# Rows of x directly ahead of the next chunk's scores in TensorE's order, from the third block on

## Chip, cores, metric

One core of a Trainium2 chip. The metric is the device time of one execution in microseconds (us); a ratio always compares kernels that ran on the same chip in the same rounds.

## The reference

A gated linear attention (4 batches, 8 heads, 768 tokens, head size 48) feeds a feed-forward block with an unusual activation:

```python
f = 1/(1+exp(-f_logit))
for t in range(S):                                   # 768 tokens
    state = f[t][:, None] * state + outer(k[t], v[t])
    y[t]  = q[t] @ state
x = y as (3072 tokens, 384)
h = x @ w_in                                         # 384 -> 2048
g = h * erf(max(h,0) + log1p(exp(-|h|)))
out = g @ w_out                                      # 2048 -> 384
```

## The kernel before

Tokens are taken in 24 chunks of 128; three chunks make one of 8 blocks, numbered 0 to 7 in the code (the "third block" is `blk == 2`, chunks 6 to 8). While the feed-forward matmuls of block `it` and `it - 2` run on TensorE as a stream of "slots" (one 128x384 program matmul each, 0.645 us), the attention of block `it + 1` is dropped in between, in four stages per chunk:

- `stage_d` (decays): one matmul `ps_d`; ScalarE exps `dp` and `kd`; VectorE makes `qd`, GpSimd makes `kd`
- `stage_t`: 8 transposes `ps_t`, copied to `qT` and `kT`
- `stage_s` (scores): 8 matmuls `sc`, masked by VectorE into `A`; 8 matmuls `dS`; VectorE and GpSimd update the state `Mbd`
- `stage_y` (rows of x): 28 program matmuls (16 in the first chunk of a batch), with 32 output columns each, copied to `xT`

In the traces the engines take their instructions in program order. The parts (cut):

```python
def prepare(blk, j0, j1):          # gates of a whole block
    nc.vector.tensor_scalar(out=lt, in0=lt, scalar1=LOGIT_MIN, ..., op0=ALU.max)
    nc.scalar.activation(out=lt, in_=lt, func=AF.Exp, scale=-1.0)
    nc.scalar.activation(out=lt, in_=lt, func=AF.Ln, bias=1.0)
...
def stages(blk):
    g0 = blk * CPB
    todo = [(stage_d, g0), (stage_t, g0)] if blk == 1 else []
    for g in range(g0, g0 + CPB):
        last = g == n_chunks - 1
        todo += [] if last else [(stage_d, g + 1)]
        todo += [(stage_s, g)]
        todo += [] if last else [(stage_t, g + 1)]
        todo += [(stage_y, g)]
    return todo
...
for it in range(n_blocks + 2):
    blk = it + 1
    todo = deque(stages(blk) if blk < n_blocks else [])
    n = n_slots[it]                            # 48, 48, then 96
    at = [int(3 + (n - 13) / max(1, len(todo)) * i) for i in range(len(todo))]
    for s, _ in enumerate(slots(it)):          # one large matmul per slot
        ...                                    # weight rounding steps (VectorE), loads
        if at and s == at[0]:
            at.pop(0); f, g = todo.popleft(); f(g)
        ...                                    # a step of the activation
        if it + 2 < n_blocks and s == (16 if it < 2 else n // 2):
            prepare(it + 2, 0, CPB)
```

In `hidden()` the copies of hidden values out of PSUM are made by ScalarE for `blk < 2` and by VectorE after that. In the profiles `hps` are the hidden values as the matmuls write them, `Hg` their copy, `ops` the output sums. In PSUM, where the matmuls write, there are two buffers for `hps` and `ops` and two ("at") that `ps_d`, `ps_t` (twice), `dS` and `y` share in turn.

Of the kernel before, what the change touches and what calls it, by code (L numbers as in the profile page):

```python
# [38 lines left out]
FP32 = mybir.dt.float32  # L39
# [4 lines left out]
ALU = mybir.AluOpType  # L44
# [24 lines left out]
P = 128  # L69
# [3 lines left out]
def kernel(  # L73
# [11 lines left out]
    B, H, S, D = q.shape  # L85
# [5 lines left out]
    HP = H // 2  # L91
# [3 lines left out]
    CPB = 3  # L95
    TB = CPB * P
    n_blocks = B * S // TB
    n_chunks = B * NCH
# [23 lines left out]
    def rows(r, n=D):  # L122
        return slice(DP * r, DP * r + n)
# [3 lines left out]
    def y_matmuls(y, A, vt, qT, Mbd):  # L127

        for kt in range(n_k):
            todo = []  # L130
            for i in range(P // M):
                a, part = divmod(kt * (P // M) + i, 3)
                pair = vt[:, a].rearrange("p r d -> p (r d)")
                heads_in = {0: (0,), 1: (0, 1), 2: (1,)}[part]
                start = {0: 0, 1: M, 2: DP + D - M}[part]
                terms = []
                for r in heads_in:
                    o = D if (part == 1 and r == 1) else start
                    terms.append((pair[:, o : o + M], A[:, r, a, :]))
                if Mbd is not None:  # L140
                    flat = Mbd[:, a].rearrange("p r d -> p (r d)")
                    terms.append((flat[:, M * part : M * (part + 1)], qT[:, a, :]))
                todo.append(terms)
            for n in range(max(len(t) for t in todo)):
                for i, terms in enumerate(todo):
                    if n < len(terms):
                        nc.tensor.matmul(  # L147
                            y[M * i : M * (i + 1), kt, :], lhsT=terms[n][0], rhs=terms[n][1],
                            start=(n == 0), stop=(n == len(terms) - 1), skip_group_check=True,
                        )  # L150
# [17 lines left out]
    work1 = main.enter_context(tc.tile_pool(name="work1", bufs=1))  # L168
# [20 lines left out]
    def load_f(g):  # L189
        b, c = divmod(g, NCH)  # L190
        blk, j = divmod(g, CPB)
        if j == 0:
            lts[blk] = lpool.tile([P, CPB, d_model], FP32, name="lt", tag="lt")
        nc.sync.dma_start(
            out=lts[blk][:, j, :].rearrange("t (h d) -> t h d", d=D), in_=heads(f_logit, b, c)
        )
# [120 lines left out]
    def keep_busy(n):  # L317

        for _ in range(n):
            nc.tensor.matmul(busy[-1], lhsT=tri[:], rhs=tri[:], start=True, stop=True)  # L320
# [48 lines left out]
    def stage_s(g):  # L369
        b, c = divmod(g, NCH)  # L370
        qT, kT = qTs[g], kTs.pop(g)
        sc = ps_sc.tile([P, 2, HP, P], FP32, name="sc", tag="sc")
        for a in range(HP):
            for r in range(2):
                nc.tensor.matmul(  # L375
                    sc[:, r, a, :], lhsT=kT[rows(r), a, :], rhs=qT[rows(r), a, :],
                    start=True, stop=True,
                )
        if g in totals:

            pairs = dps[g % 2][:].rearrange("t (a r) d -> t a (r d)", r=2)
            for a in range(HP):
                nc.tensor.matmul(
                    totals[g][:, a : a + 1], lhsT=pairs[:, a, :], rhs=ident[:, P - 1 : P],
                    start=True, stop=True,
                )
            nc.vector.tensor_copy(out=Tall[:, g, :], in_=totals.pop(g))
        A = work1.tile([P, 2, HP, P], FP32, name="A", tag="A")
        nc.vector.tensor_tensor(  # L389
            out=A[:].rearrange("s r a t -> s (r a) t"),  # L390
            in0=sc[:].rearrange("s r a t -> s (r a) t"),
            in1=tri[:].unsqueeze(1).broadcast_to((P, H, P)),
            op=ALU.mult,
        )
        As[g] = A
        if c == NCH - 1:
            return
        dS = ps_at.tile([P, HP, D], FP32, name="dS", tag="at")
        vt, kd = vts[g % NV], kds[g % 2]
        for a in range(HP):  # L400
            for r in range(2):
                h = 2 * a + r
                nc.tensor.matmul(  # L403
                    dS[rows(r), a, :], lhsT=kd[:, h, 0:D], rhs=vt[:, a, r, 0:D],
                    start=True, stop=True,
                )
        new, old = Mbds[g % 2], Mbds[(g + 1) % 2]
        Sn = work1.tile([P, HP, D], FP32, name="Sn", tag="Sn")
        for r in range(2):
            total = Tall[rows(r), g, :].unsqueeze(2).broadcast_to((D, HP, D))  # L410
            if c == 0:
                nc.vector.tensor_tensor(
                    out=new[rows(r), :, r, :], in0=dS[rows(r)], in1=total, op=ALU.mult
                )
                continue
            nc.vector.tensor_tensor(  # L416
                out=Sn[rows(r)], in0=dS[rows(r)], in1=old[rows(r), :, r, :], op=ALU.add
            )
            nc.gpsimd.tensor_tensor(  # L419
                out=new[rows(r), :, r, :], in0=Sn[rows(r)], in1=total, op=ALU.mult  # L420
            )

    def stage_y(g):
        c = g % NCH
        blk, j = divmod(g, CPB)
        if j == 0:
            xTs[blk] = work.tile([P, n_k, TB], FP32, name="xT", tag="xT")
        if blk == 0:
            keep_busy(3)
        y = ps_at.tile([P, n_k, P], FP32, name="y", tag="at")  # L430
        y_matmuls(y, As.pop(g), vts[g % NV], qTs.pop(g), Mbds[(g + 1) % 2] if c else None)
        nc.scalar.copy(out=xTs[blk][:, :, j * P : (j + 1) * P], in_=y[:])  # L432


    acts = deque()
# [108 lines left out]
    def slots(it):  # L544

        if it >= n_blocks:
            return project(it - 2)
        made = [hidden(it, gi) for gi in range(n_g)]
        return chain(*made) if it < 2 else chain(*made[:2], project(it - 2), *made[2:])
# [20 lines left out]
    with tc.manual_schedule():  # L570
# [13 lines left out]
        for g in range(CPB, 2 * CPB):  # L584
# [3 lines left out]
            out=tri[:], in_=tri[:], pattern=[[1, P]], compare_op=ALU.is_ge, fill=0.0,  # L588
# [32 lines left out]
        def load_more():  # L621
            if to_load and home_free(to_load[0]):
                load_piece(to_load.pop(0))
# [51 lines left out]

        def stages(blk):
            g0 = blk * CPB
            todo = []
            if blk == 1:
                todo = [(stage_d, g0), (stage_t, g0)]  # L680
            for g in range(g0, g0 + CPB):
                last = g == n_chunks - 1
                todo += [] if last else [(stage_d, g + 1)]
                todo += [(stage_s, g)]
                todo += [] if last else [(stage_t, g + 1)]
                todo += [(stage_y, g)]
            return todo

        check = check_decays()
# [1 line left out]
        for it in range(n_blocks + 2):  # L691
            blk = it + 1
            if it + 2 < n_blocks:
                for j in range(CPB):
                    load_f((it + 2) * CPB + j)
            todo = deque(stages(blk) if blk < n_blocks else [])
            n = n_slots[it]
            at = [int(3 + (n - 13) / max(1, len(todo)) * i) for i in range(len(todo))]
            for s, _ in enumerate(slots(it)):
                due += 1 if it == 0 and s < 36 else 0.75  # L700
                while due >= 1:
                    weights_step()
                    due -= 1
                if s % 6 == 3:
                    load_more()
                if at and s == at[0]:
                    at.pop(0)
                    f, g = todo.popleft()
                    f(g)
                    if f is stage_y:  # L710
                        load_to(g + LOOK)
                if it == 0:
                    step = s >= 16 and s % 8 == 4
                elif it == 1:
                    step = s % 8 == 4
                elif it == 2:
                    step = s % 3 == 1
                elif it < n_blocks:
                    step = s % 7 in (2, 5)
                else:  # L720
                    step = s % 3 == 2
                if step and not 66 <= s < 72:
                    act_step()
                if it + 2 < n_blocks and s == (16 if it < 2 else n // 2):
                    prepare(it + 2, 0, CPB)
                if it == n_blocks - 1 and s in (5, 40):
                    next(check)
            assert not todo
# [216 lines left out]
```

## Time and profile before

| | before |
|---|---|
| median of 3 runs (at the prediction) | 648.13 us |
| span of the profiled run | 646.4 us |
| TensorE / ScalarE / VectorE / GpSimd busy | 98 / 79 / 73 / 9% |
| busy in 75 to 145 us, of 70 us: TensorE / VectorE | 68.54 / 65.97 us |

TensorE's records overlap: that of a large matmul lasts 490 ns in the mean (page of the kernel before), while 62 of them in an undisturbed stretch start 0.3224 us apart; so what counts is the distance from one start to the next. The last row is the stretch in which the third block's attention is built: VectorE is nearly full there, because it still rounds weights (38.5 us of the 65.97). The profile lines of the kernel before stand in the prediction below.

### The profile page before, as it was taken

The page shows a single profiled execution, that of the slowest core. Times are in us where ns is not written, and L with a number is a line of the kernel's source. Part 1 is how long each engine was busy: PE and PEld are TensorE (multiplying, and loading weights), DVE is VectorE, ACT ScalarE, POOL GpSimd, SP SyncE. Part 2 cuts the span into 40 slices and gives each one's busy share as a digit, 9 for nine tenths or more (in the row PEclk, how much of TensorE's full clock was granted, in tenths as well). Part 3 has the DMA queues.
Part 4 walks back from the last instruction along what each step waited for, and adds up shares of the span by engine and source line. Part 5 has one row for each costly group of instructions (what it writes and reads, how often), then busy time and mean ns, then how long its engine had stood idle before and what let it go on. Part 6 is the DMA issues. An engine that isn't in the chain of part 4 may idle for free.

```text
span 646.4 us, 9360 instructions
## 1 busy us (share of the span) xinstructions
PE 630.7 (98%) x3815; PEld 393.8 (61%) x3815; DVE 474.6 (73%) x440; ACT 510.0 (79%) x459; POOL 59.1 (9%) x61
## 2 busy tenths in 40 slices
PE   8899999999999999999999999999999999999995
PEld 6756666665656666656656666666666655555553
DVE  4798889997777886678657687668765686577761
ACT  5446667679899888797898978978787899799971
POOL 0112101120110010201210002201020000000000
PEclk9999999999999999999999999999999999999999
DMA  9996872310113120221203211020001000000001
GB/s 192 252 269 149 220 204 50 75 24 14 37 37 74 25 38 13 62 50 25 38 13 76 45 28 24 13 75 1 1 0 38 1 0 1 37 1 0 37 1 41
DMA packets 120689, 36.90 MB, mean 57 GB/s; under 512 B 112448, under 2 KB 115520, under 8 KB 120640
## 3 DMA queue, kind: packets, MB, share of 16 engines
q1 hardware_dynamic: 118560, 35.84, 24.0%
q10 hardware_dynamic: 2080, 0.39, 0.4%
q8 instruction: 32, 0.52, 0.3%
q14 instruction: 17, 0.14, 0.1%
HBM read 31.46 MB, written 4.72 MB: 56 GB/s over the span
## 4 chain that ended last, share of the span: by engine, by line
PE 75%; ACT 12%; DVE 8%; issue 3%; DMA 1%; POOL 0%; DVEq 0%; POOLq 0%; ACTq 0%
PE hps L491 32%; PE ops L524 27%; PE y L147 5%; ACT x L153 5%; PE sc L375 4%; DVE e L158 3%; PE ps_t L357 3%; PE ps_d L330 2%; ACT yl L446 1%; ACT e L457 1%; PE dS L403 1%; ACT L297 1%; ACT e L442 1%; ACT L457 1%; DVE Hg L460 1%
## 5 line engine op out<-in xcount | busy, mean ns | idle before, releaser
L491 PE MATMUL hps<-xT,w_in_sb 128*128 128x384 f32 x768 | 259.9, 490 | 1.3 <-ACT xT L432 0.6
L524 PE MATMUL ops<-w_out_sb,Hg 128*128 128x384 f32 x768 | 256.2, 489 | 1.2 <-DVE Hg L460 1.2
L158 DVE SCALAR_TENSOR_TENSOR e<-x,e 128x1536 f32<-128x1536 f32 x128 | 230.3, 1799 | 6.3 <-DVE e L158 0.5
L153 ACT ACTIVATE x<-yl,serf_bias 128x1536 f32<-128x1536 f32 x128 | 195.0, 1566 | 14.1 <-DVE e L158 14.0
L524 PEld LDWEIGHTS ops<-w_out_sb,Hg 128*128 128x128 f32 x768 | 143.7, 190 | 99.4 <-issue 2.2
L491 PEld LDWEIGHTS hps<-xT,w_in_sb 128*128 128x128 f32 x768 | 142.5, 190 | 96.9 <-issue 2.2
L460 DVE TENSOR_TENSOR Hg<-Hg,e 128x1536 f32<-128x1536 f32 x32 | 56.5, 1765 | 63.9 <-ACT e L457 63.8
L503 DVE COPY Hg<-hps 128x768 f32<-128x768 f32 x48 | 45.7, 952 | 20.1 <-PE hps L491 19.7
L347 POOL TENSOR_TENSOR kd<-kn,kd 128x384 f32<-128x384 f32 x21 | 29.4, 1401 | 323.1 <-issue 185.7
L457 ACT ACTIVATE e<-e 128x1536 f32<-128x1536 f32 x32 | 47.5, 1483 | 10.6 <-DVE e L158 10.3
L446 ACT ACTIVATE yl<-e 128x1536 f32<-128x1536 f32 x32 | 47.5, 1485 | 0.4
L442 ACT ACTIVATE e<-Hg 128x1536 f32<-128x1536 f32 x32 | 47.3, 1477 | 0.0
L343 DVE TENSOR_TENSOR qd<-qn,dp 128x384 f32<-128x384 f32 x24 | 14.2, 591 | 36.6 <-ACT dp L333 36.6
L297 ACT ACT_TABLE_LOAD x31 | 39.8, 1283 | 1.3 <-PEq L929 0.8
L457 ACT ACT_TABLE_LOAD x31 | 39.8, 1283 | 0.5
L419 POOL TENSOR_TENSOR Mbd<-Sn,Tall 48x192 f32<-48x192 f32 x32 | 28.6, 893 | 97.0 <-DVE Sn L416 82.3
L389 DVE TENSOR_TENSOR A<-sc,tri 128x1024 f32<-128x1024 f32 x24 | 29.3, 1219 | 8.4 <-PE sc L375 8.1
L147 PE MATMUL y<-A,vt 128*32 128x128 f32 x768 | 35.2, 277 | 0.1
L147 PEld LDWEIGHTS y<-A,vt 128*32 128x32 f32 x768 | 27.4, 109 | 12.0 <-issue 4.1
L432 ACT COPY xT<-y 128x384 f32<-128x384 f32 x24 | 11.3, 472 | 26.0 <-PE y L147 25.9
L375 PEld LDWEIGHTS sc<-qT,kT 48*128 48x128 f32 x384 | 23.3, 187 | 12.5 <-issue 11.3
L147 PE MATMUL y<-qT,Mbd 128*32 128x128 f32 x480 | 30.2, 273 | 0.0
(72 smaller groups left out, 389.9 us busy)
## 6 DMA issues: line engine op xcount, KB each, us to landing
lt<-in_f_logit_dram SPq DMA_DIRECT2D x24, 192.0 KB, 4.2
qn<-in_q_dram SPq DMA_DIRECT2D x24, 192.0 KB, 3.2
Hg<-in_moe_w_out_dram SPq DMA_DIRECT2D x6, 768.0 KB, 6.3
kn<-in_k_dram SPq DMA_DIRECT2D x23, 192.0 KB, 3.2
vt<-in_v_dram SPq DMA_DIRECT2D x23, 192.0 KB, 3.1
w_out_sb<-in_moe_w_in_dram SPq DMA_DIRECT2D x4, 768.0 KB, 6.3
Hg<-in_moe_w_in_dram SPq DMA_DIRECT2D x4, 768.0 KB, 7.1
out_dram<-osb SPq DMA_DIRECT2D x8, 384.0 KB, 2.5
```

Source lines behind the costliest of these rows:

```text
L147: nc.tensor.matmul(y[M * i : M * (i + 1), kt, :], lhsT=terms[n][0], rhs=terms[n][1], start=(n == 0), stop=(n == len(terms) - 1), skip_grou ...
L153: nc.scalar.activation(out=dst[:], in_=y[:], func=AF.Square, bias=serf_bias[:, i : i + 1], scale=SERF_K)
L158: nc.vector.scalar_tensor_tensor(out=e[:], in0=x[:], scalar=SERF_AB[i][1], in1=e[:], op0=ALU.add, op1=ALU.mult)
L297: nc.scalar.add_instruction(mybir.InstLoadActFuncSet(act_func_set_id=EXP_LN, name=nc.get_next_instruction_name(), engine=mybir.EngineType. ...
L375: nc.tensor.matmul(sc[:, r, a, :], lhsT=kT[rows(r), a, :], rhs=qT[rows(r), a, :], start=True, stop=True,)
L442: nc.scalar.activation(out=e[:], in_=h, func=AF.Exp)
L446: nc.scalar.activation(out=y[:], in_=e[:], func=AF.Ln, scale=SERF_C, bias=1.0)
L457: nc.scalar.activation(out=e[:], in_=e[:], func=AF.Tanh)
L460: nc.vector.tensor_tensor(out=h, in0=h, in1=e[:], op=ALU.mult)
L491: nc.tensor.matmul(hps[:, j, 0:TB], lhsT=w_in_sb[:, kt, ft * P : (ft + 1) * P], rhs=xTs[blk][:, kt, :], start=(kt == 0), stop=(kt == n_k - 1),
L503: nc.vector.tensor_copy(out=to, in_=hps[:, :, 0:TB])
L524: nc.tensor.matmul(ops[tt // 2][:, tt % 2, 0:d_model], lhsT=gr["h"][:, j, tt * P : (tt + 1) * P], rhs=w_out_sb[:, ft, :], start=(ft == 0), ...
```

## The change

The intent is to change the shape of TensorE's matmuls less often: y (32 output columns) and the next chunk's scores (48 rows) no longer have large matmuls between them. A chunk becomes three steps instead of four, and the tile `Sn` goes. The diff is cut; left out is only that the loads ahead now also follow `stage_y_s`.

```diff
-        Sn = work1.tile([P, HP, D], FP32, name="Sn", tag="Sn")
...
             nc.vector.tensor_tensor(
-                out=Sn[rows(r)], in0=dS[rows(r)], in1=old[rows(r), :, r, :], op=ALU.add
+                out=new[rows(r), :, r, :], in0=dS[rows(r)], in1=old[rows(r), :, r, :], op=ALU.add
             )
             nc.gpsimd.tensor_tensor(
-                out=new[rows(r), :, r, :], in0=Sn[rows(r)], in1=total, op=ALU.mult
+                out=new[rows(r), :, r, :], in0=new[rows(r), :, r, :], in1=total, op=ALU.mult
             )
+    def stage_y_s(g):
+        stage_y(g)
+        stage_s(g + 1)
...
-            todo = []
             if blk == 1:
                 todo = [(stage_d, g0), (stage_t, g0)]
+                for g in range(g0, g0 + CPB):
+                    todo += [(stage_d, g + 1), (stage_s, g), (stage_t, g + 1), (stage_y, g)]
+                return todo
+            todo = [(stage_s, g0)] if blk == 2 else []
             for g in range(g0, g0 + CPB):
-                last = g == n_chunks - 1
-                todo += [] if last else [(stage_d, g + 1)]
-                todo += [(stage_s, g)]
-                todo += [] if last else [(stage_t, g + 1)]
-                todo += [(stage_y, g)]
+                if g < n_chunks - 1:
+                    todo += [(stage_d, g + 1), (stage_t, g + 1), (stage_y_s, g)]
+                else:
+                    todo += [(stage_y, g)]
             return todo
```

More of the change, by code (lines that the diff above doesn't have):

```diff
@@ L709 @@
                     f(g)
-                    if f is stage_y:
+                    if f in (stage_y, stage_y_s):
                         load_to(g + LOOK)
```

## The prediction

> **What bounds the kernel now.** I read the page first (busy shares, slices), then TensorE's waits, then TensorE's timeline of one chunk, then the timelines of ScalarE, VectorE and GpSimd around the places where TensorE stood still, and the end of ScalarE's timeline.
>
> ```profile
> PE 630.7 (98%) x3815; PEld 393.8 (61%) x3815; DVE 474.6 (73%) x440; ACT 510.0 (79%) x459; POOL 59.1 (9%) x61
> PE   8899999999999999999999999999999999999995
> ```
>
> TensorE is busy for 630.7 of 646.4 us, so at most 15.7 us of standing still could be won. By stretches of the windows view, 2.55 us lie before 8 us, 2.53 in 8 to 38, 1.74 in 38 to 75, 1.46 in 75 to 145, 0.72 in 145 to 200, none from 200 to 624, and 6.74 in the last 22. A change to blocks 3 to 8 can win little there: it must make TensorE's own stream denser. A busy sum hides gaps between pipelined matmuls, so I read distances from start to start in the timeline of TensorE. Each 128x384 program matmul appears as two.
>
> ```profile
> 251.66 0.43 PE L147 MATMUL y<-qT,Mbd 128*32 128x128 f32 x8
> 252.02 4.78 PE L524 MATMUL ops<-w_out_sb,Hg 128*128 128x384 f32 x14
> 256.64 0.81 PE L330 MATMUL ps_d<-lt,tri 128*128 128x384 f32 x2
> 257.29 4.68 PE L524 MATMUL ops<-w_out_sb,Hg 128*128 128x384 f32 x14
> 261.89 1.16 PE L375 MATMUL sc<-qT,kT 48*128 48x128 f32 x16
> 262.99 0.56 PE L403 MATMUL dS<-vt,kd 128*48 128x48 f32 x16
> 263.48 4.14 PE L524 MATMUL ops<-w_out_sb,Hg 128*128 128x384 f32 x12
> ...
> 541.84 20.16 PE L524 MATMUL ops<-w_out_sb,Hg 128*128 128x384 f32 x62
> 561.83 15.64 PE L491 MATMUL hps<-xT,w_in_sb 128*128 128x384 f32 x48
> ```
>
> The lower pair gives the undisturbed pace: (561.83 - 541.84)/62 = 0.3224 us. The 14 after the rows of x (y) last 256.64 - 252.02 = 4.62 us where 14 x 0.3224 = 4.51 would do: 0.11 us more. The 14 before the scores (sc) last 261.89 - 257.29 = 4.60: 0.09 more. So both changes of matmul shape have a price that no idle column shows.
>
> [...] y has 32-column outputs, the scores 48-row operands at two row positions, the rest full tiles[...]. In weight load's timeline the scores' first load begins with the first score matmul, at 261.89, after 0.55 us of idleness[...] the multiplication for kd takes about 1.0 us on GpSimd in some chunks and 2.61 us at 184.27, where a VectorE operation of two inputs, 1.75 us long, began at the same moment.
>
> **The change part by part.** (a) *Joins.* The order of TensorE's instructions shows y of chunk g directly ahead of the scores of g+1 for g = 6 to 22: 17 joins. Each replaces y -> large and large -> scores by one y -> scores. The prologue already has that neighbourhood:
>
> ```profile
> 25.84 0.43 PE L147 MATMUL y<-qT,Mbd 128*32 128x128 f32 x8
> 26.20 1.16 PE L375 MATMUL sc<-qT,kT 48*128 48x128 f32 x16
> 27.29 1.05 PE L383 MATMUL ps_d<-ident,dp 128*128 128x1 f32 x8
> ```
>
> From the start of y's last eight to the next matmul it is 26.20 - 25.84 = 0.36 us there and 252.02 - 251.66 = 0.36 us before large ones; the scores last 1.09 to 1.10 us in both. So y -> scores costs no more than y -> large at that spot, and the join saves 0.11 + 0.09 = 0.20 us. Another chunk gives the same (40 after y from 275.27 to 288.28: 13.01 - 12.90 = 0.11; 12 before the scores at 292.88: 3.96 - 3.87 = 0.09). 17 x 0.20 = **3.4 us off** TensorE's path.
>
> (b) *Fewer, wider steps.* A chunk is spread over three steps, not four: decays (ps_d), transposes (ps_t), then the join. In block 3, built beside the second block's 48 slots, a step is 35/10 = 3.5 slots of 0.645 us; later 83/9 = 9.2 slots. What gets nearer: decays to transposes were two steps apart with scores between (about 11.5 us from block 4 on, 6 us in block 3) and become one: 0.65 + 9 x 0.645 = 6.5 us, and in block 3 0.65 + 3 or 4 x 0.645 = 2.6 to 3.2 us to qd's transposes, 0.44 us later for kd's. What gets further: y from its masked scores (two steps to three), and the dS copy from the transposes that reuse its PSUM buffer.
>
> (c) *Sn gone.* VectorE adds straight into Mbd, GpSimd scales in place: same counts and shapes, 350 ns and 893 ns each. The last reader of that Mbd is y of the chunk before, ahead on TensorE anyway. I count **0**.
>
> **Block 3, TensorE's stalls.** TensorE's timeline shows two at the place that (b) touches:
>
> ```profile
> 92.18 0.63 PE L357 MATMUL ps_t<-ident,kd 128*128 128x128 f32 x4 [0.56 <-DVE Mbd L412]
> 117.07 0.60 PE L357 MATMUL ps_t<-ident,qd 128*128 128x128 f32 x4
> 118.57 0.63 PE L357 MATMUL ps_t<-ident,kd 128*128 128x128 f32 x4 [0.90 <-DVE Sn L416]
> ```
>
> These are waits for dS's PSUM buffer, about 2 us of VectorE work behind a crowded queue (VectorE busy 65.97 of 70 us). Now the first transposes take that buffer, some 5.2 us after dS (7 slots and the decays) rather than 3.6: 1.46 us should go. In exchange the transposes may wait for their operands. Counted from the start of the decays' matmul, qd ended at 1.93 us for the three decays of that stretch and kd at 2.8, 2.8 and 3.7 us (GpSimd's timeline gives the last):
>
> ```profile
> 87.16 1.01 POOL L347 TENSOR_TENSOR kd<-kn,kd 128x384 f32<-128x384 f32 x1 [17.67 <-ACT kd L336]
> 99.55 0.99 POOL L347 TENSOR_TENSOR kd<-kn,kd 128x384 f32<-128x384 f32 x1 [11.38 <-ACT kd L336]
> 112.62 1.81 POOL L347 TENSOR_TENSOR kd<-kn,kd 128x384 f32<-128x384 f32 x1 [6.84 <-issue]
> ```
>
> Against kd's due time of 3.0 to 3.7 us that is 0 to 0.6 us per chunk; and VectorE, nearly full here, sets a pace that TensorE can't outrun. I take 1.0 us back: net **-0.4 us**. From block 4 on the slowest were kd at 7.2 us (decays at 179.64) and 6.1 us (334.13) against 6.9 allowed: I add **+0.3 us**.
>
> **The end.** Past 562 us ScalarE, not TensorE, carries the chain: it runs almost without a pause from 562.5 to 626 us. Would TensorE's gain pass through?
>
> ```profile
> 555.58 1.46 ACT L442 ACTIVATE e<-Hg 128x1536 f32<-128x1536 f32 x1
> 559.45 0.80 ACT L531 COPY osb<-ops 128x768 f32<-128x768 f32 x1 [2.42 <-PE ops L524]
> 562.03 0.48 ACT L536 COPY osb<-ops 128x384 f32<-128x384 f32 x1 [1.78 <-PE ops L524]
> ```
>
> ScalarE waits 2.42 and 1.78 us there, both for TensorE's ops, with the run of 64 us queued behind. So even if ScalarE came no earlier, up to 4.2 us pass, more than my sum. **Sum:** 648.13 - 3.4 - 0.4 + 0.3 = 644.6; with a little of the block 3 joins lost to VectorE's pace, **644.8 us**.
>
> **The rivals.** First: *the shorter way from decays to transposes becomes the wait.* For it: in-order TensorE, ScalarE busy 51.4 of 55 us in 145 to 200, and a decay's exp that began 3.65 us after its matmul at 179.64. Against it: 16 of the 24 chunks have that exp within 0.9 us, and most have kd by 3.7. If every chunk of block 3 lost 1.5 us and some later ones 0.5, the time would be 647 to 649. Second: *TensorE isn't the bound where it gains*: ScalarE or VectorE sets the pace, and the gain turns into idleness before Hg's product or at the end. For it: ScalarE's run after 562 us, VectorE's share before 145. Against it: TensorE never stands still from 200 to 624 us, and the 4.2 us above. It would give 646.5 to 648. [...]
>
> **Range and chances.** The joins are countable and seen twice, so the spread is from the waits: -1.5 to +3 us. I give 643.0 to 647.2 eight times in ten. Two per cent is 13 us; nothing above comes near either way: faster by over 2% 0.01, within 2% 0.98, slower by over 2% 0.01.
>
> **What would show it.** Right: 128x384 runs before y still cost their bit, but no large matmul stands between y and sc; the scores start about 0.36 us after y's last eight; pieces of TensorE's stream per chunk sum to 0.2 us less; the waits for Mbd and Sn at the transposes are gone. Wrong: transposes waiting for kd on GpSimd or qd on VectorE by over 2 us in total; ScalarE no longer waiting near 557 to 562 us while the span is unchanged; a longer idleness than 1.25 us before the last 24 ops matmuls; or scores that start later than 0.36 us after y.

## The result, and the profile after

| | before | after |
|---|---|---|
| median of 6 runs | 648.12 us | 653.01 us |
| ratio, 95% interval | | 1.0071 (1.0059 to 1.0084) |
| span profiled | 646.4 us | 650.7 us |

A ratio is the mean time of one kernel's fast runs over that of the other's of the same rounds, so it isn't quite the ratio of the medians quoted. By the medians the change costs 4.9 us where 3.3 us of gain were predicted. From the page of the kernel after, the busy line and the slices (one digit per 16.3 us, in tenths; PEclk is the granted TensorE clock):

```profile
PE 630.0 (97%) x3815; PEld 396.2 (61%) x3815; DVE 476.1 (73%) x440; ACT 509.6 (78%) x459; POOL 56.3 (9%) x61
...
PE   8999997998999999999999999999999999999995
...
PEclk9999998999999999999999999999999999999999
```

The seventh slice, 98 to 114 us, has fallen to 7 and its clock to 8; the tenth (146 to 163 us) is below 9 too. Everything later is as full as before. The list of TensorE's waits (us in total, times, longest) names the new ones:

```profile
PE ps_t L357 <- DVE qd L343: 4.0, 4, 3.0
PE hps L495 <- DVE Hg L507: 2.6, 2, 2.3
...
PE ps_t L357 <- POOL kd L347: 1.0, 1, 1.0
```

**The joins work.** TensorE's timeline of a later chunk (start, duration, line, what, number of matmuls):

```profile
310.81 0.43 PE L147 MATMUL y<-qT,Mbd 128*32 128x128 f32 x8
311.17 1.16 PE L375 MATMUL sc<-qT,kT 48*128 48x128 f32 x16
```

The scores start 0.36 us after y's last eight, as in the prologue. To date gains and losses I numbered the 1536 records of large matmuls in program order and subtracted their start times, after minus before. At equal places of successive blocks (numbers 412, 604, 796) the difference is +7.66, +7.07, +6.48 us: 0.6 us won in each block of three joins, 0.20 us per join.

**The loss comes all between 84 us and the next block's first matmuls.** The difference is +0.60 us from the first of these matmuls, at 32 us, to the 101st at 84 us. That is scatter of the start: in the experiments' profiles it lies between -0.3 and +0.65 us with no relation to the edit. By the 149th, at 118 us, it is +7.78 us (some 1.7 of them because at that place one more chunk's scores have been done), and from the 1133rd to the end +4.35 us. TensorE's timeline around chunk 8's decays and transposes (the bracket is idleness just before, and what ended it):

```profile
101.62 0.81 PE L330 MATMUL ps_d<-lt,tri 128*128 128x384 f32 x2
102.26 2.10 PE L495 MATMUL hps<-xT,w_in_sb 128*128 128x384 f32 x6
107.39 0.63 PE L357 MATMUL ps_t<-ident,qd 128*128 128x128 f32 x4 [3.03 <-DVE qd L343]
109.02 0.66 PE L357 MATMUL ps_t<-ident,kd 128*128 128x128 f32 x4 [1.00 <-POOL kd L347]
109.52 4.44 PE L495 MATMUL hps<-xT,w_in_sb 128*128 128x384 f32 x8
```

TensorE stands still for 3.03 and 1.00 us. Then eight large matmuls take 4.4 us where 8 x 0.3224 = 2.6 would do. VectorE's timeline has qd waiting for the exp (dp), and ScalarE's tells why that was late:

```profile
106.69 0.56 DVE L343 TENSOR_TENSOR qd<-qn,dp 128x384 f32<-128x384 f32 x1 [3.03 <-ACT dp L333]
...
103.22 1.16 ACT L311 ACTIVATE lt<-lt 128x1152 f32<-128x1152 f32 x1 [5.26 <-DVE lt L307]
104.42 1.16 ACT L312 ACTIVATE lt<-lt 128x1152 f32<-128x1152 f32 x1
105.48 0.78 ACT L505 COPY Hg<-hps 128x768 f32<-128x768 f32 x1
106.17 0.49 ACT L333 ACTIVATE dp<-ps_d 128x384 f32<-128x384 f32 x1
```

The exp of chunk 8's decays (dp) could have begun at about 102.5 us (0.85 us after its matmul, as in the kernel before: 98.60 - 97.75); it began at 106.17, behind the fourth block's preparation (lt), which itself waited in ScalarE's order for VectorE, which was behind with its work. In the kernel before, chunk 8's decays are placed at slot 14 and the preparation at 16; with three steps per chunk the decays move to slot 17, behind it. ScalarE in the kernel before has the two in the other order:

```profile
98.60 0.49 ACT L333 ACTIVATE dp<-ps_d 128x384 f32<-128x384 f32 x1 [0.80 <-PE ps_d L330]
...
102.06 1.17 ACT L311 ACTIVATE lt<-lt 128x1152 f32<-128x1152 f32 x1 [2.59 <-DVE lt L307]
```

Windows of 2 us of the kernel after (busy us and instructions of TensorE, weight loads, VectorE, ScalarE, GpSimd, then the granted clock, and the DMA's share and rate) explain the slow matmuls:

```profile
110.00:112.00 2.00, 2.00 (x4) 1.00 (x3) 1.97 (x3) 1.69 (x2) 0.00 (x0) 0.50 0.80 158
112.00:114.00 2.00, 2.00 (x9) 0.97 (x11) 1.48 (x2) 0.65 (x1) 0.00 (x0) 0.75 0.20 39
```

After the stall the clock is granted at half, for 3.41 us: the windows view reads 0.50 over 109.58 to 112.99 us and 1.00 on either side. The idleness before it comes in two pieces, 3.03 and 1.00 us, and some 5.2 us pass from one large matmul to the next, with two sets of transposes (0.63 and 0.66 us) among them; which of these brings the clock down is not shown here.

The second wait is at the border to the next stretch. TensorE, then VectorE:

```profile
148.37 0.91 PE L495 MATMUL hps<-xT,w_in_sb 128*128 128x384 f32 x2 [2.26 <-DVE Hg L507]
```

```profile
145.11 0.55 DVE L343 TENSOR_TENSOR qd<-qn,dp 128x384 f32<-128x384 f32 x1
145.57 1.75 DVE L158 SCALAR_TENSOR_TENSOR e<-x,e 128x1536 f32<-128x1536 f32 x1
147.36 0.96 DVE L507 COPY Hg<-hps 128x768 f32<-128x768 f32 x1
```

The decays of chunk 10 began at 140.14 and their exp at 140.99, yet VectorE reaches qd only at 145.11: it is over 3 us behind, and the first hidden copy that falls to it comes so late that TensorE has no PSUM buffer free.

**The end passes everything through**, as predicted: ScalarE still waits 2.41 us there for TensorE. The gains of the experiments pass too (experiment 12: -5.07 us at the 1133rd matmul and -5.06 at the last).

```profile
563.80 0.80 ACT L535 COPY osb<-ops 128x768 f32<-128x768 f32 x1 [2.41 <-PE ops L528]
```

The sum for the profiled pair: waits of TensorE after 75 us 0.31 + 3.03 + 1.00 + 0.28 + 2.26 + 0.35 = 7.2 us against 0.56 + 0.90 + 0.33 + 0.39 = 2.2 before (the 1.25 us near the end are in both): +5.0. Half clock: 4.37 us from the first of the eight matmuls to y, less 2.58 and the usual 0.1: +1.7. Joins 17 x 0.20: -3.4. Start: +0.6. Together +3.9 of +4.35 us.

### The profile page after: what moved, and what is told of

Its sections match the earlier page's. It is cut to its first block, busy times and chain, and to the rows that moved or that the text cites. A ratio compares the mean times of both kernels' runs of the same rounds, so it can differ in the third digit from the quotient of the medians.

```text
span 650.7 us, 9345 instructions
## 1 busy us (share of the span) xinstructions
PE 630.0 (97%) x3815; PEld 396.2 (61%) x3815; DVE 476.1 (73%) x440; ACT 509.6 (78%) x459; POOL 56.3 (9%) x61
## 4 chain that ended last, share of the span: by engine, by line
PE 77%; ACT 10%; DVE 7%; issue 3%; DMA 1%; SPq 1%; POOL 1%; DVEq 0%; POOLq 0%
PE ops L528 30%; PE hps L495 29%; PE y L147 6%; PE sc L375 4%; ACT x L153 4%; PE ps_t L357 3%; DVE e L158 3%; PE ps_d L330 2%; ACT e L461 1%; PE dS L403 1%; ACT yl L450 1%; DMA lt<-in_f_logit_dram 1%; ACT L297 1%; ACT e L446 1%; DVE Hg L464 1%
## 5 line engine op out<-in xcount | busy, mean ns | idle before, releaser
L347 POOL TENSOR_TENSOR kd<-kn,kd 128x384 f32<-128x384 f32 x21 | 31.2, 1487 | 227.9 <-ACT kd L336 148.6
L418 POOL TENSOR_TENSOR Mbd<-Mbd,Tall 48x192 f32<-48x192 f32 x32 | 23.9, 747 | 197.4 <-DVE Mbd L415 158.1
L333 ACT ACTIVATE dp<-ps_d 128x384 f32<-128x384 f32 x24 | 11.7, 488 | 25.9 <-PE ps_d L330 25.8
```

Source lines behind the costliest of these rows:

```text
L347: (nc.vector if blk == 0 else nc.gpsimd).tensor_tensor(out=kd, in0=kns[g % NQ][:].rearrange("t (h d) -> t h d", d=D), in1=kd, op=ALU.mult)
```

## The experiments

The theory after the result (A): the preparation's collision with chunk 8's exp, made harmful by the shorter step. Its rivals: the three-step spacing is too short by itself (B); the later blocks lose too (C). For the second wait (D): VectorE's backlog at the border. Medians of 4 runs (5 for the last) and ratios to the kernel before of the same rounds. Experiments 1 to 4, 5 to 8, 9 to 11 and 12 ran in four sets of rounds on four chips, in which the kernel before had medians of 648.12, 648.30, 647.98 and 648.22 us; where experiments of different sets are compared below, a difference of a few tenths of a us decides nothing. In the second and third set two of the seven runs of the kernel before took 650.6 to 650.9 us, which widens those intervals. The ratios of all experiments are within 2% of the kernel before; the differences of interest are smaller than that, so the intervals and the profiles are what decides.

### 1. Preparation moved behind chunk 8's transposes

```diff
-                if it + 2 < n_blocks and s == (16 if it < 2 else n // 2):
+                if it + 2 < n_blocks and s == (16 if it == 0 else 21 if it == 1 else n // 2):
```

> The changed kernel, but the preparation of the fourth block's gates (two ScalarE passes over lt, behind one VectorE pass) is emitted at slot 21 of the third block's stretch instead of slot 16, so that it comes behind the decays and transposes of chunk 8 and not directly ahead of its exps. Theory A (collision: chunk 8's exp of the decays queues behind this preparation, and the step to the transposes is now too short to hide it): the 3.03 and 1.00 us stalls at chunk 8's transposes and the 1.75 us of halved clock after them go, and with them most of the 2.26 us wait for the Hg copy later; 653.0 - 5.8 = 647.2 us, down to 645 us if the later wait goes too. Theory B (the three-step spacing of 3 to 4 slots is too short by itself, any chunk's exps come too late): the stall only moves, time stays at 651 us or above.

Measured: 648.32 us, ratio 0.9992 (0.9976 to 1.0009). The kernel after was timed in other rounds, in which the kernel before had the same median of 648.12 us; beside its 653.01 us this is 4.7 us less. It is 1.1 us above the 647.2 expected; the low clock after the later wait, told below, is enough for that (0.66 on the mean of 143 to 148 us; by my estimate from it, 5 x 0.34 = 1.7 us). TensorE's timeline:

```profile
104.24 0.60 PE L357 MATMUL ps_t<-ident,qd 128*128 128x128 f32 x4
105.47 0.66 PE L357 MATMUL ps_t<-ident,kd 128*128 128x128 f32 x4 [0.62 <-POOL kd L347]
...
143.17 0.91 PE L495 MATMUL hps<-xT,w_in_sb 128*128 128x384 f32 x2 [2.30 <-DVE Hg L507]
```

Chunk 8's stall is gone (0.62 us left), and the slow pace after it: the eight large matmuls take 2.68 us to y, against 4.37. B falls as the main cause: the steps are just as short. The later wait didn't go, it is 2.30 us now, and the clock after it fell to 0.50 (windows view, 145 to 147 us). Such a low clock is not certain: one of the four runs took 646.52 us at a mean clock of 0.999, the others 648.2 to 648.9 at 0.996.

### 2. The third block in the old order

```diff
-            if blk == 1:
-                todo = [(stage_d, g0), (stage_t, g0)]
+            if blk < 3:
+                todo = [(stage_d, g0), (stage_t, g0)] if blk == 1 else []
...
-            todo = [(stage_s, g0)] if blk == 2 else []
+            todo = [(stage_s, g0)] if blk == 3 else []
```

> The changed kernel, but the third block keeps the old four-step order; joins only from chunk 9 on (14 of the 17). Both theories: all the loss was in the third block's stretch, so it goes; the 14 joins at 0.20 us each stay: 648.1 - 2.8 = 645.3 us (644.8 to 646.0). If instead part of the loss comes from the blocks from the fourth on (theory C: fewer, wider steps cost there too), 647 us or more.

Measured: 645.42 us, ratio 0.9955 (0.9939 to 0.9972). As expected; C falls. From the 101st large matmul on, the difference to the kernel before goes from +0.21 to -2.57 us: 2.8 us for 14 joins.

### 3. The collision alone, in the kernel before

```diff
-                if it + 2 < n_blocks and s == (16 if it < 2 else n // 2):
+                if it + 2 < n_blocks and s == (16 if it == 0 else 13 if it == 1 else n // 2):
```

> The kernel before, with only the preparation of the fourth block's gates moved from slot 16 to slot 13 of the third block's stretch, so that it stands directly ahead of chunk 8's decays as in the changed kernel, but with six slots and the scores between decays and transposes. Theory A in its full form (collision and short step are needed together): chunk 8's exp comes 3 to 4.5 us late, but 5 to 6 us lie between decays and transposes; 0 to 1.5 us slower, 648 to 649.6 us, without the halved clock. Theory A' (the collision alone does it): 651 to 653 us.

Measured: 651.04 us, ratio 1.0040 (1.0023 to 1.0056). It is at the edge of A', well over A's 649.6: the long step does not hide the collision. Chunk 8's exp began 3.58 us after its matmul, and qd was ready at 4.65 us, before its transposes at 6.30; but this wait came out elsewhere:

```profile
106.54 0.63 PE L357 MATMUL ps_t<-ident,kd 128*128 128x128 f32 x4 [2.07 <-DVE Sn L416]
```

In VectorE's order the sums that free dS's PSUM buffer stand behind qd, which was ready at those 4.65 us and not at 1.93 as in the kernel before; they came so late that TensorE waited 2.07 us for them. The clock fell after this as well, to 0.62 in 107 to 109 us and then 0.52:

```profile
109.00:111.00 2.00, 2.00 (x15) 0.81 (x17) 1.97 (x3) 0.57 (x2) 0.00 (x0) 0.52 0.00 0
```

This low clock is the profiled run's (651.74 us, mean clock 0.995); the other three runs, at 0.997 to 1.000, still took 650.25 to 651.25 us. So my theory needs mending: the collision costs 2.9 us in the old order as well; in the new order, with its shorter step, it costs the 4.7 us of experiment 1.

### 4. TensorE kept busy during the stall

```diff
             flat = src[:].rearrange("t (a r) d -> t a (r d)", r=2)
+            if g == 8 and src is qd:
+                for _ in range(24):
+                    nc.tensor.matmul(ps[:, 0, :], lhsT=tri[:], rhs=tri[:], start=True, stop=True)
```

> The changed kernel with 24 needless 128x128 matmuls ahead of chunk 8's transposes of qd, written to the PSUM tile which the transposes then overwrite. They fill about 2.6 of the 3.03 us in which TensorE stood still there. If the 1.75 us in which the following large matmuls ran at a granted clock of about 0.5 come from that idleness, they go: 653.0 - 1.75 = 651.3 us (650.9 to 651.8), with the stall itself unchanged. If the low clock has another cause, 653 us.

Measured: 652.27 us, but from 650.81 to 655.22 in four runs; the time decides nothing. The profile of the 650.81 us run does: the eight matmuls ran at full pace, 2.68 us from the first to y, against 4.37 us after the change, where the clock was 0.66 in 109 to 114 us. The dummies filled 5.4 us rather than 2.6, longer than the stall, and took some of the gain back. In this execution the slow pace did not appear once the idleness was filled; the same 2.29 us wait at the border remained.

### 5. One large matmul between y and scores

Built on experiment 2:

```diff
     def stage_y_s(g):
         stage_y(g)
-        stage_s(g + 1)
+        late.append(g + 1)
...
+                while late:                       # at the next slot, behind its large matmul
+                    stage_s(late.pop())
                 if at and s == at[0]:
```

> The kernel with the old order in the third block and joins from chunk 9 on (645.4 us), with exactly one large program matmul put between each of its 14 y and the scores that follow; nothing else. If the saving of a join lies in the two changes of matmul shape that it drops (0.11 + 0.09 us), all of it is lost: 14 x 0.20 = 2.8 us more, 648.2 us (647.6 to 648.8). If the gain came from the wider steps or from y's later place instead, it stays at 645.4 us.

Measured: 649.15 us (648.31 to 651.45), ratio 0.9998 (0.9968 to 1.0028). All of the gain is lost (the time is 0.35 us above the range expected). The profiled run was the slowest, with a wait of 2.09 us at 60 us and a low clock (0.79 on the mean of 58 to 66 us); from the 101st large matmul to the end its difference to before goes from +2.78 to +3.20, so it is 3.2 us worse than experiment 2 there, 0.23 us for each of 14 joins. TensorE's timeline shows the price whole:

```profile
308.44 0.91 PE L497 MATMUL hps<-xT,w_in_sb 128*128 128x384 f32 x2
309.29 1.16 PE L375 MATMUL sc<-qT,kT 48*128 48x128 f32 x16
```

The pair between y and scores takes 0.85 us instead of 0.645: 0.20 us for the two changes of shape.

### 6. Only Sn taken out of the kernel before

```diff
-        Sn = work1.tile([P, HP, D], FP32, name="Sn", tag="Sn")
-                out=Sn[rows(r)], in0=dS[rows(r)], ...
+                out=new[rows(r), :, r, :], in0=dS[rows(r)], ...
-                out=new[rows(r), :, r, :], in0=Sn[rows(r)], in1=total, ...
+                out=new[rows(r), :, r, :], in0=new[rows(r), :, r, :], in1=total, ...
```

> The kernel before with only the tile Sn taken out: VectorE adds straight into Mbd and GpSimd scales it in place. Both theories: no effect, 648.1 us (647.6 to 648.6); if the in-place product or the strided destination costs something, it shows here alone.

Measured: 648.19 us, ratio 0.9982 (0.9952 to 1.0012). No effect.

### 7. Two hidden copies of the third block on ScalarE

On experiment 1's kernel:

```diff
-                        if blk < 2:
+                        if blk < 2 or (blk == 2 and gi == 0):
                             nc.scalar.copy(out=to, in_=hps[:, :, 0:TB])
```

> The changed kernel with the fourth block's preparation at slot 21 (648.3 us), and the first two copies of hidden values of the third block done by ScalarE rather than VectorE. Theory D: the 2.3 us wait of the hidden matmuls at 143 us is VectorE's backlog at the border of the two stretches, which reaches the first of these copies; with ScalarE, nearly idle there, it goes, and with it the low clock after it (up to 1.9 us in some runs): 644.5 to 646 us. If the wait comes from something else (the PSUM buffers being held longer by TensorE's own order) it stays at 648 us.

Measured: 644.17 us (643.78 to 644.61), ratio 0.9925 (0.9896 to 0.9955), 4.1 us better than experiment 1 and just below the range expected. The wait of 2.30 us is gone from TensorE's timeline, and the runs' mean clocks are 0.998 to 0.999. This supports theory D, with the low clock that followed the wait: 2.3 us of wait and the 1.7 us estimated for the clock in experiment 1 make 4.0 of the 4.1. ScalarE was not idle there (busy for 3.97 of the 4 us from 139 to 143 us in experiment 1), and the wait went all the same.

### 8. Chunk 9's scores set apart again

On experiment 1's kernel:

```diff
+                if g == 8:
+                    todo += [(stage_d, g + 1), (stage_t, g + 1), (stage_y, g)]
+                elif g == 9:
+                    todo += [(stage_d, g + 1), (stage_s, g), (stage_t, g + 1), (stage_y_s, g)]
-                if g < n_chunks - 1:
+                elif g < n_chunks - 1:
```

> The changed kernel with the preparation at slot 21, and with chunk 9's scores set apart from chunk 8's y and put back to where the kernel before has them, behind chunk 10's decays: 16 joins. If the 2.3 us wait at the border comes from the mask product and the Mbd sums of chunk 9 (1.23 + 0.73 us on VectorE) being moved ahead into the stretch where VectorE is full, the wait falls to 0.3 us as in the kernel before, 648.3 - 2.0 - (0 to 1.9 of low clock) + 0.2 = 645 to 646.5 us. If chunk 9's share isn't the cause, 648.5 us.

Measured: 645.31 us, ratio 0.9942 (0.9913 to 0.9971), 3.0 us better than experiment 1 with one join fewer; the wait for Hg's copy is gone from the list. So the work of chunk 9's scores on VectorE (1.23 + 0.73 us), pulled ahead into the full stretch, is what made the first copy late.

### 9. The copies alone

On the changed kernel, the preparation left at slot 16:

```diff
-                        if blk < 2:
+                        if blk < 2 or (blk == 2 and gi == 0):
                             nc.scalar.copy(out=to, in_=hps[:, :, 0:TB])
```

> The changed kernel with the preparation left at slot 16, and only the first two copies of hidden values of the third block given to ScalarE. If the two waits are separate terms of the sum, only the later one (2.26 us) goes: 653.0 - 2.3 = 650.7 us (650.0 to 651.3). If the later wait is only an echo of the first (VectorE idle for 3 us while it waited for chunk 8's exp, and late ever after), ScalarE's copy hides the echo and the same number comes out, but then moving the preparation alone should have removed it too, which it did not; so a time below 649 us would say that the terms are not additive.

Measured: 649.45 us, ratio 1.0011 (0.9977 to 1.0046). That is 3.6 us better than the kernel after's 653.01, more than the 2.3 expected. In the profiles the difference to before, from the 101st large matmul to the end, goes down from 3.76 to 1.24 us, so 2.5 us; the stall at chunk 8 is unchanged (3.04 and 1.00 us). The further 1.1 us of the medians are not accounted for by these two profiles; 0.3 of them is the start's scatter, and the kernel after's profiled run was its fastest (652.49 us, mean clock 0.996; four of the other five had 0.993 or 0.994), so low clock after the second wait in the other runs is likely, but I have no trace of those.

### 10. The old order in the third block, and the copies

On experiment 2's kernel:

```diff
-                        if blk < 2:
+                        if blk < 2 or (blk == 2 and gi == 0):
                             nc.scalar.copy(out=to, in_=hps[:, :, 0:TB])
```

> The old order in the third block, joins from chunk 9 on (645.4 us), with the first two copies of hidden values of that block on ScalarE. The 0.76 us wait for VectorE's copy at 145 us goes: 644.7 us (644.2 to 645.2). Against the 17-join version with both repairs (644.2 us) it tells whether joining inside the third block is worth anything: 3 x 0.2 us against waits of 1.2 us for chunks 7 to 9's operands less 1.5 us of waits for dS's buffer; the expectation is 0.5 us for joining.

Measured: 644.20 us, ratio 0.9931 (0.9897 to 0.9964): the median of experiment 7, from other rounds. From the 101st large matmul to the end the profile gains 3.7 us on the kernel before, experiment 7's 4.0 us. So joining inside the third block is worth some 0.3 us at most, which these runs don't tell from nothing (0.5 us were expected): waits for qd and kd there, 0.31 + 0.63 + 0.31 us in experiment 7, take most of what the joins and the freed dS buffer (0.56 + 0.91 us of waits here) give.

### 11. The three-step order in the second block too

On experiment 7's kernel:

```diff
             if blk == 1:
-                todo = [(stage_d, g0), (stage_t, g0)]
-                for g in range(g0, g0 + CPB):
-                    todo += [(stage_d, g + 1), (stage_s, g), (stage_t, g + 1), (stage_y, g)]
-                return todo
-            todo = [(stage_s, g0)] if blk == 2 else []
+                todo = [(stage_d, g0), (stage_t, g0), (stage_s, g0)]
+            else:
+                todo = []
...
-                ... s == (16 if it == 0 else 21 if it == 1 else n // 2):
+                ... s == (24 if it == 0 else 21 if it == 1 else n // 2):
```

> The 17-join version with both repairs (644.2 us), with the new three-step order in the second block too (three more joins) and the third block's preparation at slot 24 of that stretch. Gains: 3 x 0.2 us and the 1.6 and 0.4 us waits for dS's buffer in it; losses: transposes waiting for qd and kd in steps of 2.9 slots, 0.3 to 0.9 us a chunk. Net expected 642.5 to 645; if VectorE, full there as well, sets the pace, 644 to 646.

Measured: 650.11 us, ratio 1.0023 (0.9989 to 1.0058). A miss by 5 us. TensorE's timeline, and GpSimd's:

```profile
53.75 1.12 PE L357 MATMUL ps_t<-ident,kd 128*128 128x128 f32 x4 [6.23 <-POOL kd L347]
```

```profile
51.55 1.08 POOL L418 TENSOR_TENSOR Mbd<-Mbd,Tall 48x192 f32<-48x192 f32 x2 [13.64 <-DVE w_in_sb L286]
```

The multiplication for kd stood behind a state product in GpSimd's order, which began at 51.55 us. In the kernel before, the product there began no sooner (52.75 us, its profile names the small DMAs into Tall, issued from 47.27 us on behind the loads of gates), but the decays that needed GpSimd next came later. A low clock came with the wait (0.91 on the mean of 36 to 75 us, windows view): the six large matmuls behind it took 2.96 us where 6 x 0.3224 = 1.93 would do. The same kind of fault as at chunk 8: an in-order engine held by something that the shorter step brought in front. That the DMAs are the cause in this kernel too is read from the kernel before, not shown.

### 12. Decays one or two slots earlier

On experiment 7's kernel:

```diff
             at = [int(3 + (n - 13) / max(1, len(todo)) * i) for i in range(len(todo))]
+            if it == 1:
+                assert at == [3, 6, 10, 13, 17, 20, 24, 27, 31, 34], at
+                at = [3, 5, 10, 13, 15, 20, 24, 26, 31, 34]
```

> The 17-join version with both repairs (644.2 us), with the decays of chunks 7, 8 and 9 issued one or two slots earlier (slots 5, 15 and 26 of the third block's stretch rather than 6, 17 and 27), so that five slots of large matmuls, not three or four, lie between them and the transposes: 0.65 + 5 x 0.645 = 3.9 us to qd's and 4.3 us to kd's. Measured in the version with the preparation moved: qd ready at 2.0, 3.5 and 3.5 us, kd at 3.1 to 3.8 us after the decays began. If the short step is what makes the transposes wait (0.31, 0.62, 0.28 and 0.17 us), these go: 644.2 - 1.3 = 642.9 us (642.4 to 643.6). If VectorE's pace is the limit in that stretch, the waits move to another place and the time stays at 644.2 us.

Measured: 643.28 us (642.93 to 643.52), ratio 0.9923 (0.9910 to 0.9937), the best of all. The waits for qd and kd in the third block (0.31, 0.62 and 0.28 us in experiment 1) are gone; a new one of 0.23 us appeared (decays for the copy of xT that frees their PSUM buffer).

## Why the prediction was wrong

- **Joins, 3.4 us: right.** 0.20 us each, in the profile after and by experiments 2 and 5.
- **Sn, 0: right** (experiment 6). **The end, right:** the whole difference of +4.35 us before the end is there at the end.
- **"From block 4 on ... +0.3 us": right in size by luck.** The reason given, late kd, did not come: decays to transposes never stalled there. One wait of 0.35 us for a hidden copy at 217 us happens to be as long.
- **"Block 3 ... net -0.4 us": this is the step that failed.** In its place the runs show 4.03 us of stall at chunk 8 alone. The removed waits for dS's buffer did go (1.46 us). The short step by itself cost about what I took: 0.31 + 0.28 us in the kernel after beside chunk 8, and 0.31 + 0.62 + 0.28 = 1.2 us in experiment 1, against 1.0; only at chunks 7 and 9 it was qd that was late and not kd: they had it 3.5 us after the decays began, not 1.93, because VectorE's queue had not come to it (the exps began after 0.85 us as before). But the working took the exps' delay from the kernel before ("kd at 2.8, 2.8 and 3.7 us") and asked only how many slots lay between. It did not ask what else had a fixed slot: the preparation at slot 16 used to come after chunk 8's decays and now came before them. Chunk 8's exp began 4.55 us after its matmul instead of 0.85, and experiments 1 and 3, which move nothing but the preparation, take this away and bring it about. My first rival had the right wait, "the shorter way from decays to transposes becomes the wait", but for a general reason that experiment 1 refutes as the main one, and with about half the size (647 to 649 us against 653).
- **VectorE's pace, "a little of the block 3 joins lost": mis-sized.** Pulling chunk 9's scores ahead across the border put 1.96 us of work into a stretch with 4 us of slack in 70, and TensorE waited 2.26 us at the next copy (experiments 7 and 8).
- **Not in the prediction at all: the half clock.** It added 1.7 us to 4.0 us of stall in the profiled run.

## What to carry to other kernels

When a change moves stages among fixed slots, list everything else that has a slot on the engines in between (preparations, copies, loads), and check what each in-order queue now has ahead of the instruction that matters; a latency measured in the old order need not hold in the new one (0.85 us became 4.55 here). A saving on the busiest engine of 0.2 us a time is real, but one wait of 3.03 us with the 1.7 us of half clock behind it eats twenty-three; here the same change with the preparation moved by five slots and two copies given to ScalarE (experiment 7) gains 0.75% instead of losing 0.71%. Work pulled ahead across a border between stages should be counted against the fullest engine of the stage it lands in.

## What the traces show of changes of shape and of the clock

- Two changes (32-column to full, full to two 48-row positions) cost 0.20 us: in experiment 5 the pair between y and the scores takes 0.85 us instead of 0.645. Going straight from the 32-column to the 48-row shape shows no cost of its own: the scores start 0.36 us after y's last eight (310.81 and 311.17 us in the kernel after), as large matmuls do (251.66 and 252.02 us in the kernel before), and the join saves the whole 0.20 us. What costs the time inside TensorE is not shown.
- Waits of 2.07 us (experiment 3) and 2.30 us (experiment 1) were followed by a granted clock of 0.52 (109 to 111 us) and 0.50 (145 to 147 us), and the wait of 2.09 us in experiment 5 lies in a stretch with a mean clock of 0.79 (58 to 66 us), while the 2.26 us wait of the kernel after's profiled run was not followed by a low clock (1.00 in 146 to 152 us). No run here separates what tells these waits apart.
